# Pooled attention and a residual MLP on one core: batch 0's prologue regrouped, batch 1's v loaded in another shape, PSUM split into three pools

## The chip, the cores and the metric

The kernel runs on one core of one Trainium2 chip. The core has TensorE (PE, matrix products), VectorE (DVE), ScalarE (ACT), GpSimd (POOL) and SyncE (SP), each with its own instruction stream that it works through in order, and DMA engines that all of them share. Times are microseconds on the device. The metric is the time of one execution, lower is better.

## The reference, cut to what matters

There are 8 batches, 8 heads, 576 tokens and 64 values a head. Keys and values are averaged over groups of 8 tokens, so each query attends to 72 groups. Attention's output, 576 x 512 for a batch, then goes through a residual MLP that mixes tokens first and channels second:

```python
k_p = k.reshape(B, H, 72, 8, D).mean(axis=3);  v_p = v.reshape(B, H, 72, 8, D).mean(axis=3)
attn = softmax(scale * q @ k_p.T);  x = (attn @ v_p) laid out as (B, 576, 512)
a1 = alpha1 * x + beta1
u = x + lam * einsum('ts,bsd->btd', w_tok, a1)
a2 = alpha2 * u + beta2
out = u + lam * (relu(a2 @ w_ch1) @ w_ch2)      # 512 -> 2048 -> 512
```

Inputs and outputs are fp32. The products run in bf16 or fp16 with fp32 sums.

## The kernel before, in words

**Stages.** The tokens of a batch are cut into four chunks of 128 rows (token 4p + c lies on partition p of chunk c) and a remainder of 64; the remainders of two batches share a chunk. Four chunks make a block of the MLP, so there are nine blocks. A prologue (lines 659 to 748) does the attention and the token mix of batch 0 and prepares `w_tok`, biases and constants. Then block n of the MLP runs while the attention and the mix of batch n + 1 are woven into it.

**What sets the order.** Nothing is scheduled by a tool. The prologue is a written list of calls. In the loop over blocks each piece of work has a due number (`todo.append((at, ...))`), the list is sorted, and the pieces are issued in that order. Within a block, numbers 0 to 15 are the 16 columns of the first layer (`mlp_A`, L603), 16 to 31 are the 16 parts of the second layer (`mlp_B`, L619). Each engine follows its own stream; a wait at one instruction holds all that stand behind it on that engine.

**Attention of a batch.** `att_F` (L353) transposes q: for batches 0 and 1 by TensorE, later by DMA. `att_K` (L396) pools k with products by `pool_main` and `pool_rem`. For batch 0, `att_S` (L447) makes the scores of one head in two column halves and takes their exponentials; it uses `kpT_pool`, where the two halves of the partitions are kept apart with zeros. For the other batches `att_S4` (L463) makes four heads at once from `kp_pool`, with two half-array products side by side, and six exponentials (L503). For batch 0, `first_V` (L423) pools v by products of a 16-bit copy; for the others `att_V` (L438) adds fp32 v, eight tokens a partition on 72 partitions, in three VectorE sums a head pair (L442, L444). `att_AV` (L507) multiplies exponentials by pooled v (L518, L522); a column of eights beside v gives the sum for the division (L524, L526). `att_X` and `rest_X` (L536, L529) multiply by lambda times alpha1 and give `xs` in bf16, heads two by two.

**Mix and MLP.** `mix_T` (L565) multiplies the transposed `w_tok` by `xs` in five products of 512 columns (L572), adds x (L576), and multiplies by alpha2 (L579, `u_bf`). `mix_uT` (L581) transposes `u_bf` into `u_fm`: by TensorE for block 0, by DMA later. `mlp_A` is four products (L609) and a relu on ScalarE (L614). `mlp_B` is four products a part (L643) and, after the fourth part, two VectorE operations (L649, L650) and the store.

**Constants.** `spread_lam` (L275) copies lambda to all partitions by a K=1 product, `spread_al1` (L281) multiplies it by alpha1, `load_al2` (L271) broadcasts alpha2 by DMA from SP's queue. `setup_wtok` (L293), `setup_rowsum` (L306), `setup_vectors` (L288) and `setup_bias` (L343) prepare the transposed `w_tok`, its row sums and the biases. `keep_warm` (L559) issues products of 512 columns whose result nobody reads.

**Buffers and queues.** PSUM has eight banks. Six are the pool `psA` (`gp`, L52), handed out in turn to whatever asks; two are `psB`. A tile must wait until the last reader of the tile that held its bank is done. Loads that change the type go through POOL's queue, in the order of POOL's stream; stores, fp32 loads and DMA transposes go through SP's.

Of the kernel before, what the change touches and what calls it, by code (L numbers as in the profile page):

```python
# [14 lines left out]
P = 128  # L15
# [8 lines left out]
def kernel(  # L24
# [24 lines left out]
    psA = ctx.enter_context(tc.tile_pool(name="psA", bufs=6, space=bass.MemoryType.PSUM))  # L49
    psB = ctx.enter_context(tc.tile_pool(name="psB", bufs=2, space=bass.MemoryType.PSUM))  # L50

    def gp(name):  # L52
        return psA.tile([P, 512], FP, tag="gp", name=name)

# [61 lines left out]

    def load_rem(b, queue=nc.sync, behind=None):
# [52 lines left out]
    def load_wtok():  # L170
        nc.gpsimd.dma_start(out=wt_bf[:, 0:4 * S],
                            in_=moe_w_tok[0:512, :].rearrange("(p c) s -> p (c s)", c=4))
        nc.vector.memset(wt_bf[:, 5 * S:], 0.0)
        nc.vector.memset(wt_bf[64:128, 4 * S:5 * S], 0.0)
        nc.gpsimd.dma_start(out=wt_bf[0:REM, 4 * S:5 * S], in_=moe_w_tok[512:576, :])

# [3 lines left out]
    b2row = const.tile([4, P], FP, tag="b2row", name="b2row")  # L180
# [18 lines left out]
    nc.scalar.dma_start(out=b2row, in_=moe_beta2.rearrange("(c p) -> c p", p=P))  # L199
# [32 lines left out]
    vp1_pool, kpT_pool, kp_pool, ET_pool = [], [], [], []  # L232
    for i in range(4):
# [3 lines left out]
        if i < 2:  # L237
            t = const.tile([P, 2, 4, SPG], BF, tag=f"kpT_{i}", name=f"kpT_{i}")
            nc.vector.memset(t, 0.0)
            kpT_pool.append(t)  # L240
# [15 lines left out]
    def bias_row(i):  # L256
        p0 = 64 - 64 * i
        nc.vector.tensor_tensor(out=xs_pool[i][p0:p0 + 1, 4, :], in0=vecs[p0:p0 + 1, 1],
                                in1=vecs[p0:p0 + 1, 0], op=ALU.mult)

    b2c_bf = const.tile([P, 4], BF, tag="b2c_bf", name="b2c_bf")
    wtT = const.tile([P, 6, 640], BF, tag="wtT", name="wtT")
# [8 lines left out]
    def load_al2(behind):  # L271
        behind.memset(al2_bc[:, 0:1], 0.0)
        nc.sync.dma_start(out=al2_bc, in_=moe_alpha2.unsqueeze(0).to_broadcast((P, DM)))

    def spread_lam():  # L275

        ps = gp("ps_bc")
        nc.tensor.matmul(out=ps, lhsT=ones_row, rhs=vecs[0:1, 0])
        nc.scalar.copy(out=lam_bc, in_=ps)

    def spread_al1(half):  # L281

        ps = gp("ps_bc")[:, 0:256]
        cols = slice(256 * half, 256 * half + 256)
        nc.tensor.matmul(out=ps, lhsT=ones_row, rhs=vecs[0:1, 2, cols])  # L285
        nc.vector.tensor_tensor(out=lamal_bc[:, cols], in0=lam_bc[:, cols], in1=ps, op=ALU.mult)

    def setup_vectors():  # L288
        ps = gp("ps_vec")
        nc.tensor.transpose(out=ps[:, 0:4], in_=b2row, identity=identity[0:4, 0:4])  # L290
        nc.scalar.copy(out=b2c_bf, in_=ps[:, 0:4])

    def setup_wtok(tcx, copy):  # L293
# [4 lines left out]
        ps_w = gp("ps_w").bitcast(BF)  # L298
# [7 lines left out]
    def setup_rowsum(tcx):  # L306
# [3 lines left out]
        ps = gp("ps_rs")  # L310
# [32 lines left out]
    def setup_bias(g):  # L343
        ps_bias = gp("ps_bias")
# [8 lines left out]
    def att_F(b, hp, copy=nc.scalar.copy):  # L353
# [11 lines left out]
        ps_q = gp("ps_q").bitcast(BF)  # L365
# [30 lines left out]
    def att_K(b, u, copy):  # L396

        st = st1[b]
        ps_kp = gp("ps_kp")
# [18 lines left out]
        for a in range(2):  # L418
            rows = slice(64 * a, 64 * a + 64)
            (copy or (nc.scalar.copy, nc.vector.tensor_copy)[a])(  # L420
                out=kpT_pool[u][rows, a], in_=kp[rows])

    def first_V(b, u, copy=nc.vector.tensor_copy):  # L423
# [5 lines left out]
        for c in range(4):  # L429
            nc.tensor.matmul(out=vp, lhsT=pool_v, rhs=main[:, heads, c], start=(c == 0), stop=False)  # L430
        for c in range(2):
            nc.tensor.matmul(out=vp, lhsT=pool_vr, rhs=rest[:, heads, c], start=False,
                             stop=(c == 1))
# [13 lines left out]
    def att_S(b, h):  # L447
        st = st1[b]
        u, r, hh = h // 4, h // 2 % 2, h % 2
        ET = ET_pool[u][:, h % 4]  # L450
        for half in range(2):
            n0, n = 256 * half, 256 + 64 * half
            ps_sc = gp("ps_sc")
            nc.tensor.matmul(out=ps_sc[0:SPG, 0:256], lhsT=kpT_pool[u][:, half, h % 4, :],  # L454
# [406 lines left out]
```

The softmax here doesn't subtract the row's maximum and nothing guards it: scores larger than these inputs give would overflow.

## Time and profile before

The median of three runs is 346.46 us (346.36 to 346.72). The profiled execution took 345.48 us, and its span on the core is 343.8 us.

| Part of the profile | Reading |
|---|---|
| TensorE busy | 337.1 us, 98% of the span |
| VectorE, ScalarE, GpSimd busy | 224.7, 146.9, 90.2 us |
| Chain that ended last | PE 95%, of it first layer 36%, second layer 35%, token mix 11% |
| DMA | 45.77 MB, 133 GB/s over the span; 193 to 266 GB/s from 6.5 to 69.4 us |
| TensorE clock granted | 1.00 in every stage |

To read it: busy time of TensorE is modelled and includes the time in which a product drains, so it is checked against the distance between starts. The chain of work that ended last runs from the end backwards to whatever released each step. The stages of the table of windows were cut by hand: batch 0's attention (to 19.8 us), batch 0's mix (to 33.8), block 0's first layer, and so on.

### The profile page before, as it was taken

The numbers are of one execution on the slowest core, as the hardware profiler recorded it, in microseconds if no ns is written. First come the engines' busy times: TensorE is split into PE (matmuls) and PEld (weight loads), VectorE is DVE, ScalarE is ACT, GpSimd is POOL, SyncE is SP. The second block draws the span as 40 slices with busy tenths as digits, with TensorE's granted clock in tenths as the row PEclk, the third lists the DMA queues.
The fourth block names the chain that finished last, engine by engine and source line by source line (L and its number), as shares of the span: only waits on it lengthen the run. The fifth ranks groups of instructions, "written<-read, shape, count | busy, mean of one in ns | idle before, by whom it ended". The sixth has DMA issues, their size and how long they took to land.

```text
span 343.8 us, 5902 instructions
## 1 busy us (share of the span) xinstructions
PE 337.1 (98%) x2221; PEld 177.4 (52%) x2221; DVE 224.7 (65%) x476; ACT 146.9 (43%) x277; POOL 90.2 (26%) x105
## 2 busy tenths in 40 slices
PE   8999999999999999999999999999999999999995
PEld 3667654455445544555445544554455445545544
DVE  6664579985787667866867598768675881037511
ACT  3655980068205830385028500880089006604700
POOL 8768507201144012701170117002600200000000
PEclk9999999999999999999999999999999999999999
DMA  8999999968678907794479437982810132011012
GB/s 123 184 222 287 215 202 248 188 139 130 161 210 172 194 2 192 150 225 54 129 200 213 65 110 179 204 131 63 241 41 1 48 76 78 0 61 62 2 54 68
DMA packets 66654, 45.77 MB, mean 133 GB/s; under 512 B 34457, under 2 KB 57373, under 8 KB 66626
## 3 DMA queue, kind: packets, MB, share of 16 engines
q1 hardware_dynamic: 51716, 32.73, 40.2%
q0 software_dynamic: 14448, 12.40, 22.6%
q8 instruction: 17, 0.28, 0.3%
q10 hardware_dynamic: 462, 0.27, 0.3%
q14 instruction: 11, 0.09, 0.1%
HBM read 38.30 MB, written 9.44 MB: 139 GB/s over the span
## 4 chain that ended last, share of the span: by engine, by line
PE 95%; DMA 2%; ACT 1%; DVE 1%; issue 0%; ACTq 0%; POOLq 0%
PE ps_h L609 36%; PE ps_ch L643 35%; PE ps_tok L572 11%; PE ps_s L474 2%; PE ps_av L518 2%; DMA q_bf<-in_q_dram 2%; PE ps_ch L632 1%; PE ps_kp L404 1%; PE ps_warm L563 1%; PE ps_q L367 1%; PE ps_sc L454 1%; PE ps_r L481 1%; PE ps_av L522 1%; PE ps_bias L348 0%; PE ps_bc L285 0%
## 5 line engine op out<-in xcount | busy, mean ns | idle before, releaser
L614 ACT ACTIVATE Hj<-ps_h,bias_cols 128x512 bf16<-128x512 f32 x144 | 98.3, 689 | 164.4 <-PE ps_h L609 163.1
L609 PE MATMUL ps_h<-u_fm,w 128*128 128x512 bf16 (+1 forms) x592 | 133.3, 374 | 0.2 <-ACT u_fm L595 0.2
L643 PE MATMUL ps_ch<-w,Hj 128*128 128x512 bf16 x560 | 130.9, 379 | 0.0
L609 PEld LDWEIGHTS <-w 128*128 128x128 bf16 x592 | 63.8, 114 | 51.7 <-issue 3.0
L643 PEld LDWEIGHTS <-Hj 128*128 128x128 bf16 x560 | 52.9, 98 | 61.6 <-issue 1.6
L572 PE MATMUL ps_tok<-xs,wtT 128*128 128x512 bf16 (+3 forms) x200 | 44.9, 380 | 0.3 <-DVE xs L540 0.3
L649 DVE TENSOR_TENSOR ps_ch<-lam_bc,ps_ch 128x512 f32<-128x512 f32 x32 | 22.2, 693 | 33.3 <-PE ps_ch L643 33.0
L540 POOL TENSOR_TENSOR xs<-x_tm,lamal_bc 128x512 bf16<-128x512 f32 x10 | 12.7, 1269 | 112.5 <-DVE x_tm L526 110.4
L576 DVE TENSOR_TENSOR u_sb<-x_tm,ps_tok 128x512 f32<-128x512 f32 (+1 forms) x40 | 27.4, 684 | 10.6 <-PE ps_tok L572 10.5
L524 DVE RECIPROCAL rec<-ps_av 128x5 f32<-128x5 f32 x64 | 12.2, 191 | 32.5 <-PE ps_av L522 32.4
L526 DVE TENSOR_TENSOR x_tm<-ps_av,rec 128x320 f32<-128x320 f32 x64 | 31.5, 492 | 2.7
L650 DVE TENSOR_TENSOR u_sb<-u_sb,ps_ch 128x512 f32<-128x512 f32 x35 | 24.0, 687 | 13.6 <-PE ps_ch L643 12.5
L503 ACT ACTIVATE ET<-ps_s 72x512 f16<-72x512 f32 x56 | 32.3, 592 | 0.0
L442 DVE TENSOR_TENSOR v_u<-v_u 72x512 f32<-72x512 f32 (+1 forms) x56 | 30.8, 550 | 1.0
L572 PEld LDWEIGHTS <-wtT 128*128 128x128 bf16 (+3 forms) x200 | 17.4, 100 | 21.3 <-issue 1.7
L579 DVE TENSOR_TENSOR u_bf<-u_sb,al_bc 128x512 bf16<-128x512 f32 x34 | 26.7, 785 | 1.7 <-DMA u_fm<-u_bf 0.6
L162 POOL TENSOR_TENSOR k_raw<-k_raw 128x512 f32<-128x512 f32 x14 | 18.3, 1310 | 9.1 <-DMA k_raw<-in_k_dram 6.5
L164 POOL TENSOR_TENSOR k_bf<-k_raw 128x512 bf16<-128x512 f32 x14 | 18.4, 1318 | 1.1
L518 PEld LDWEIGHTS <-ET 72*128 72x128 f16 x256 | 14.1, 97 | 8.7 <-DVE vp L435 0.2
L79 POOL DMA_DIRECT2D q_bf<-in_q_dram x16 | 12.6, 788 | 16.7 <-DVE v_u L136 15.2
L540 DVE TENSOR_TENSOR xs<-x_tm,lamal_bc 128x512 bf16<-128x512 f32 x22 | 15.4, 701 | 0.7
L518 PE MATMUL ps_av<-vp,ET 72*128 72x66 f16 x256 | 15.8, 193 | 0.0
(121 smaller groups left out, 214.9 us busy)
## 6 DMA issues: line engine op xcount, KB each, us to landing
out_dram<-u_sb SPq DMA_DIRECT2D x32, 256.0 KB
k_raw<-in_k_dram SPq DMA_DIRECT2D x12, 512.0 KB
v_u<-in_v_dram SPq DMA_DIRECT2D x12, 512.0 KB
q_bf<-in_q_dram POOLq DMA_DIRECT2D x16, 256.0 KB, 6.6
w<-in_moe_w_ch_dram POOLq DMA_DIRECT2D x8, 512.0 KB, 14.6
v_u<-in_v_dram POOLq DMA_DIRECT2D x2, 576.0 KB, 15.1
k_raw<-in_k_dram POOLq DMA_DIRECT2D x2, 512.0 KB, 15.9
rem_raw<-in_q_dram SPq DMA_DIRECT2D x15, 64.0 KB
```

What stands on the lines that cost most here:

```text
L442: nc.vector.tensor_tensor(out=t[:, :, 0:n], in0=t[:, :, 0:n], in1=t[:, :, n:2 * n], op=ALU.add)
L503: nc.scalar.activation(out=o, in_=i, func=AF.Exp, bias=0.0, scale=0.125)
L518: nc.tensor.matmul(out=av[:, odd + c, :], lhsT=ET[:, m0:m0 + 128], rhs=vp1[:, hh, :])
L526: nc.vector.tensor_tensor(out=x[:, 1 - odd:6 - odd, dd:dd + D], in0=av[:, :, 0:64], in1=rec.unsqueeze(2).to_broadcast((P, 5, D)), op=ALU.mult)
L540: eng.tensor_tensor(out=xs[:, 0:4, cols], in0=x[:, 1:5, cols], in1=lamal_bc[:, cols].unsqueeze(1).to_broadcast((P, 4, D * (h1 - h0))), op= ...
L572: nc.tensor.matmul(out=ps_tok[p0:p1], lhsT=wtT[0:kk, at, P * c:P * c + p1 - p0], rhs=xs_pool[i][0:kk, sc, :], start=(sc == 0), stop=(sc == 4))
L576: nc.vector.tensor_tensor(out=s["u"][p0:p1, :], in0=x[p0:p1, 1 + c if c < 4 else 5 - 5 * i, :], in1=ps_tok[p0:p1, 0:DM], op=ALU.add)
L579: eng.tensor_tensor(out=s["u_bf"], in0=s["u"], in1=al2_bc, op=ALU.mult)
L609: nc.tensor.matmul(out=ps_h[:, t0:t1], lhsT=w1_of(cc, j), rhs=u_fm[n][:, cc, t0:t1], start=(cc == 0), stop=(cc == 3))
L614: nc.scalar.activation(out=t, in_=ps_h, func=AF.Relu, bias=bias_cols[:, j:j + 1], scale=1.0)
L643: nc.tensor.matmul(out=ps, lhsT=Hj[n, j][:, 128 * m:128 * m + 128], rhs=w2[j // 4][:, j % 4, :], start=(j == 0), stop=(j == NJ - 1))
L650: nc.vector.tensor_tensor(out=u, in0=u, in1=ps, op=ALU.add)
```

## The change

Four things change together.

1. **Batch 0's attention.** `att_S` and `kpT_pool` go; batch 0 uses `att_S4`, heads 0 to 3 and then 4 to 7, with all six exponentials of a group directly behind. `att_AV` comes in the order 2, 3, 0, 1, 4 to 7. Lambda times alpha1 is multiplied in one row first and then spread (`spread_lamal`). The token mix of batch 0 is cut into column halves, heads 0 to 3 and 4 to 7 (`mix_half`, eight times four products of 256 columns), and the fifth product of each chunk comes after (`mix_T`). Chunks 1 and 3 are transposed as fp32 and scaled by alpha2 in the copy (`mix_uT_fp`). There are 22 unread products instead of 16, twelve of them at the start.
2. **Batch 1's v.** It is loaded as fp32 with four tokens a partition (`load_v32`; the last 64 tokens with two), VectorE adds four to one (`sum_v`), and `first_V` pools the result by two products for four heads. In block 0 the heads of batch 1 come later (dues 14.0 to 19.0 instead of 11.9 to 18.7), the second layer's first two parts are done for all four chunks before the rest, and batch 1's own chunks are transposed by TensorE.
3. **Loads.** alpha2 goes into POOL's queue behind `w_tok`; lambda is broadcast by SP's queue. Batch 1's k, both last quarters of w1, and batch 1's v move in POOL's stream.
4. **PSUM.** `psA` has four banks, `psB` two, and a new `psX` two, which take the scores' second pairs, `mlp_B`'s chunks 2 and 3, heads 2 and 3 of the later batches and several set-up tiles.

```diff
-    psA = ctx.enter_context(tc.tile_pool(name="psA", bufs=6, space=bass.MemoryType.PSUM))
+    psA = ctx.enter_context(tc.tile_pool(name="psA", bufs=4, space=bass.MemoryType.PSUM))
     psB = ctx.enter_context(tc.tile_pool(name="psB", bufs=2, space=bass.MemoryType.PSUM))
+    psX = ctx.enter_context(tc.tile_pool(name="psX", bufs=2, space=bass.MemoryType.PSUM))
...
+    def load_v32(b):
+        main = work.tile([P, H, 4, D], FP, tag="v_u", bufs=2, name="v_main")
+        rest = work.tile([32, H, 2, D], FP, tag="v_u", bufs=2, name="v_rest")
+        nc.gpsimd.dma_start(out=main.rearrange("p h c d -> p h (c d)"),
+                            in_=v[b, :, 0:512, :].rearrange("h (p c) d -> p h (c d)", c=4))
...
+    def sum_v(b, u):
...
+        m = main[:, 4 * u:4 * u + 4]
+        nc.vector.tensor_tensor(out=m[:, :, 0:2], in0=m[:, :, 0:2], in1=m[:, :, 2:4], op=ALU.add)
+        nc.vector.tensor_tensor(out=vs[:, 4 * u:4 * u + 4, 0], in0=m[:, :, 0], in1=m[:, :, 1],
+                                op=ALU.add)
...
+        nc.gpsimd.dma_start(out=al2_bc, in_=moe_alpha2.unsqueeze(0).to_broadcast((P, DM)))
...
+    nc.vector.tensor_tensor(out=vecs[0:1, 2], in0=vecs[0:1, 2], in1=vecs[0:1, 0], op=ALU.mult)
...
+    def load_lam(behind):
+        behind.memset(lam_bc[:, 0:1], 0.0)
+        nc.sync.dma_start(out=lam_bc, in_=moe_lam.unsqueeze(0).to_broadcast((P, DM)))
+
+    def spread_lamal(half, copy):
+        ps = bp("ps_bc")[:, 0:256]
+        cols = slice(256 * half, 256 * half + 256)
         nc.tensor.matmul(out=ps, lhsT=ones_row, rhs=vecs[0:1, 2, cols])
+        copy(out=lamal_bc[:, cols], in_=ps)
...
+        ps_av = (xp if b > 1 and h in (2, 3) else gp)("ps_av")
...
+    def mix_half(c, half):
+        if half == 0:
+            ps_mix[c] = gp("ps_tok")
+        cols = slice(256 * half, 256 * half + 256)
+        for sc in range(4):
+            nc.tensor.matmul(out=ps_mix[c][:, cols], lhsT=wtT[:, sc, P * c:P * c + P],
+                             rhs=xs_pool[0][:, sc, cols], start=(sc + half == 0), stop=False)
...
+    def mix_uT_fp(c):
+        ps = xp("ps_uT")
...
+            nc.tensor.transpose(out=ps[:, 128 * cc:128 * cc + 128],
+                                in_=st2[0, c]["u"][:, 128 * cc:128 * cc + 128], identity=identity)
...
+            nc.vector.tensor_scalar(out=u_fm[0][:, cc, 128 * c:128 * c + 128],
+                                    in0=ps[:, 128 * cc:128 * cc + 128],
+                                    scalar1=al2c[:, cc:cc + 1], scalar2=None, op0=ALU.mult)
...
-        if blk:
+        if key[0] > 1 or key == (0, 4):
             nc.sync.dma_start_transpose(out=u_fm[blk][:, :, 128 * at:128 * at + 128],
                                         in_=s["u_bf"])
...
     new_batch(1)
     for g in range(2):
         load_w1(g)
+    bias_row(0, nc.gpsimd)
     load_q_bf(1, 0)
     load_q_bf(1, 1)
-    for u in range(2):
-        load_k(1, u, queue=nc.gpsimd)
-    keep_warm(3)
-    spread_lam()
-    keep_warm(3)
+    keep_warm(12)
     att_F(0, 0)
     att_F(0, 1)
     cast_rem(0, nc.vector)
+    spread_lamal(0, nc.scalar.copy)
...
+    scores(0)
     first_V(0, 0)
     double_k(1)
+    spread_lamal(1, nc.scalar.copy)
+    att_AV(0, 2)
+    att_K(0, 1, None)
+    att_F(0, 2, bank=xp)
+    att_F(0, 3, nc.vector.tensor_copy, xp)
+    att_AV(0, 3)
+    att_X(0, 2, 4, nc.gpsimd)
+    scores(1)
...
+    mix_uT_fp(1)
+    setup_bias(0, bp)
     mix_uT((0, 0))
+    mix_uT_fp(3)
     mlp_A(0, 0, 0, 256)
     mix_uT((0, 2))
...
-            for i, dt in enumerate((2.9, 3.4, 4.6, 5.1) if u else (5.7, 6.2, 2.9, 3.4)):
+            late = ((6.0, 6.5, 5.0, 5.5), (3.9, 4.4, 4.9, 5.4))[u]
+            for i, dt in enumerate(late if first else (2.9, 3.4, 4.6, 5.1) if u else (5.7, 6.2, 2.9, 3.4)):
...
+        if first:
+            for u in (0, 2, 1):
+                todo.append((11.0 + 0.1 * u, lambda u=u: sum_v(b, u)))
+            for u in range(2):
+                todo.append((13.2 + 1.0 * u, lambda u=u: first_V(b, u)))
...
-            at = 21.0 + 1.3 * c
+            at = (21.7 if first else 21.0) + 1.3 * c
...
-                at = 16 + 4 * m + part
+                at = 16 + (4 * part + m if n == 0 and part < 2 else 4 * m + part)
+                if n == 0 and part > 1:
+                    at = 24 + 2 * m + part - 2
```

## The prediction

> **What bounds the kernel now.** I read the page's first part, then the waits of TensorE, then the table of stages, then single stretches of the timeline.
>
> ```profile
> PE 337.1 (98%) x2221; PEld 177.4 (52%) x2221; DVE 224.7 (65%) x476; ACT 146.9 (43%) x277; POOL 90.2 (26%) x105
> PE ps_warm L563 <- DVE warm L201: 1.4, 1, 1.4
> PE ps_rs L312 <- ACT wtT L303: 0.3, 1, 0.3
> PE ps_tok L572 <- DVE xs L540: 0.3, 1, 0.3
> PE ps_h L609 <- ACT u_fm L595: 0.2, 1, 0.2
> ```
>
> TensorE is the bound, and its waits add up to almost nothing. A share of busy time flatters it, so I checked the starts: five products of 512 columns take 1.08 us of the chain (0.216 each), and from 33.8 us on the starts follow at that pace with some 0.3 us lost. So after the prologue every added product lengthens the kernel, and only the prologue (to 33.8) has air in it. The stages:
>
> ```profile
> 6.50:19.80 13.30, 12.83 (x140) 9.00 (x141) 8.73 (x31) 8.07 (x23) 9.78 (x13) 1.00 1.29 193
> 19.80:33.80 14.00, 13.16 (x160) 10.21 (x157) 8.27 (x16) 8.02 (x18) 11.21 (x14) 1.00 1.21 266
> 33.80:46.20 12.40, 12.40 (x131) 7.72 (x129) 6.47 (x16) 11.50 (x26) 5.66 (x7) 1.00 1.10 214
> 46.20:55.20 9.00, 8.93 (x76) 4.79 (x76) 8.26 (x29) 4.59 (x10) 2.08 (x2) 1.00 1.11 222
> 55.20:69.40 14.20, 14.20 (x71) 6.28 (x70) 12.87 (x18) 0.00 (x0) 6.54 (x7) 1.00 0.99 197
> ```
>
> Columns are stretch, PE, PEld, DVE, ACT, POOL, clock, DMA share, GB/s. The reader should see two things: DMA is full through all of it, and VectorE is nearly full (8.26 of 9.00) just ahead of 55.2. The timeline shows how near that is:
>
> ```profile
> 33.82 0.61 PE L367 MATMUL ps_q<-identity_bf,q_bf 128*128 128x128 bf16 x8
> 44.13 0.30 PE L518 MATMUL ps_av<-vp,ET 72*128 72x66 f16 x4
> 53.50 0.18 DVE L524 RECIPROCAL rec<-ps_av 128x5 f32<-128x5 f32 x1
> 53.72 0.49 DVE L526 TENSOR_TENSOR x_tm<-ps_av,rec 128x320 f32<-128x320 f32 x1
> 54.25 0.69 DVE L540 TENSOR_TENSOR xs<-x_tm,lamal_bc 128x512 bf16<-128x512 f32 x1
> 55.18 1.24 PE L572 MATMUL ps_tok<-xs,wtT 128*128 128x512 bf16 x5
> 69.44 4.48 PE L609 MATMUL ps_h<-u_fm,w 128*128 128x512 bf16 x20
> ```
>
> Batch 1's last `xs` ends at 54.94 and the product that needs it starts at 55.18. That is 0.24 us of slack. I call 33.82 S (four feed-forward columns of block 0 and the first two biases are issued, batch 1's q transposes begin), 44.13 the first attention product of batch 1, 55.18 M (its first token mix), 69.44 the end of block 0.
>
> [...]
>
> **The prologue.** Twelve unread products replace six and a K=1 product: 1.40 + 12 x 0.43 = 6.56 at most, and q lands at 1.31 + 5.17 = 6.48, so nothing moves. The K=1 product of 256 columns (0.62, L285) now stands before the remainder transposes and the row product before the cast (0.68, L258 shape); the first scores start at 10.5 instead of 9.87[...]. This hardly matters, because two landings pin what follows: the second q at 6.83 + 6.6 = 13.4 and `w_tok` at 8.29 + 9.2 = 17.5. Scores in fours make twelve exponentials of sixteen; a half takes ScalarE 2 x 0.175 + 4 x 0.48 by their starts at 76.6 and 86.9. The halves' scores start at 10.5 and, behind the second q (0.45 for transposes, 0.2, a 0.59 copy), at 14.6; the last exponential ends at 17.4, and the `w_tok` transposes start at 17.65 instead of 19.76. The sums for `xs` don't hold the mixing: POOL issues its loads until 14.3 (al2's 0.57, the bias row's 1.3 at most, and q, whose issue waits for an earlier landing as it does at 12.35 today), then makes heads 2 and 3 from 15.45, heads 0 and 1 until 18.8, heads 4 and 5 until 20.1; VectorE makes the last pair until 20.8. The first half is mixed from 19.1, the second from 21.5.
> From there to S TensorE has: transposes of `w_tok` 5 x 0.28 = 1.4; two heads 0.3; mixing in halves 8 x 0.44 + 4 x 0.22 = 4.4; row sums 4 x 0.28 = 1.1; vectors 0.2; fp32 transposes 8 x 0.15 = 1.2; biases 2 x 0.53 = 1.1; bf16 transposes 2 x 0.22 = 0.4; feed-forward 32 x 0.109 = 3.5. Sum 13.6. An fp32 transpose of this size is not in the trace: not under the bf16 one's 0.055, not over the 0.31 between fp32 passes of 256 columns (L285); I take 0.15 from the small one (L290), keeping 0.4 to 2.5 for eight. Waits: 0.4 for `ps_vec`, whose bank is freed by the third of four 0.69 us copies on ScalarE; 0.4 for the second fp32 set, whose bank is freed when VectorE has made four scaled copies (1.0 by L435's 0.24 spacing, the nearest row) behind the fourth residual add; some 0.3 of hand-overs. S = 17.65 + 13.6 + 1.1 = 32.3. Range 30.9 (no wait, cheapest transposes) to 33.1. Gain 1.5.
>
> **Block 0.** Added on TensorE after S: batch 1's v pooled by products, four of 256 columns with two changes of row count each side, 4 x 0.107 + 4 x 0.09 = 0.8; sixteen transposes of `u_bf` that DMA did before, 16 x 0.055 = 0.9. S to the first pooling product: as before from 33.82 to 46.27, less two heads (0.3) and a mode change: 12.1. So 44.4.
> Does v arrive? Before: second k 15.36 + 15.9 = 31.3, third w1 quarter 34.4, v 36.7 and 39.7, last w1 quarter 41.9. Now the last quarter (2.2) is ahead of v and one more 256 KB broadcast is under way (alpha2 joins POOL's queue ahead of w1, lambda takes its place on SP's): 256 KB at 266 GB/s, 1.0. v as 128-partition rows like k (512 KB in 1.4 to 1.9) takes 3.3 instead of 5.3. Landing 31.3 + 1.0 + 3.1 + 2.2 + 3.3 + 0.4 = 41.3, ends 40.3 and 43.0. VectorE then adds 2 x (0.69 + 0.42) + 0.69 = 2.9: ready at 44.2, just in time. Behind that wait on VectorE stand only v's copies and the heads, so nothing else is held.
> First head of batch 1: 44.4 + 0.4 + scores 0.9 + one column 0.86 = 46.55. From here two engines race to M. TensorE has eight heads 8 x 0.15, pooling 0.4, one column 0.86, six parts of the second layer 6 x 0.864 = 5.2: 7.7. VectorE's work before, from 44.49 to 54.94, was 10.45; less 0.23 idle and less `att_V`'s last pair (0.68 + 0.42 + 0.29, 1.48 by starts) it is 8.74; two new v copies bring 0.48, and the first evacuation starts 0.36 after its head: 9.6. M = 56.15. **TensorE waits 1.9 us there**: the later heads removed columns that had covered VectorE.
> M to the end was 14.26; with the transposes 15.1. End of block 0: 71.25 against 69.44, **+1.8**. Check by terms: -1.5 + 0.8 + 0.9 + 1.9 - 0.3 (block 0's old losses).
>
> **Later blocks, at nothing.** With four banks in the first pool, column j7 needs the bank whose relu ended at 75.86 + 0.69 = 76.55; it starts at 76.63. All other tiles of a block have more. The two scores' halves and the third and fourth output chunk alternate in the new pool with 10 us between. The reordered second layer, four open sums, has its last weights 2.5 us and more before use. POOL's k sums (35.1 and 38.2, behind six load issues) are ready 1.0 and 0.4 ahead of their products.
>
> The sum stands against its own span of 343.8; the three timed runs are 346.36 to 346.72, so I add 1.8 to their median: 348.3.
>
> **Rivals.**
> 1. VectorE doesn't bind at M[...]. Then M comes at 46.55 + 7.7 and the sum is -0.1: 346.4, no change. For: TensorE waits nowhere on VectorE there today. Against: 0.24 us of slack today and 2.9 us less cover.
> 2. Faster: the prologue gives more. Work after 17.5 could be 13.0 with no wait, S = 30.5 at best, and if M isn't bound either, 67.6 + 0.0: 344.6. With the wait at M it turns faster only with S before 30.4.
> 3. v lands at 43.0 or later: pooling waits until 45.9, and everything behind it shifts by 1.5: 349.8. For: DMA share above 1.1 throughout.
> 4. The banks do bind: 0.1 to 0.2 us at j7 and j14 in seven blocks, +1.5 on top, 349.8. Against: each release above precedes its use.
>
> **How the numbers follow.** Theory 0.60 (alone 347.2 to 349.2: S from 30.9 to 33.1 moves it, v's readiness damps the low side), rival 3 0.11, rival 4 0.05, rival 1 0.13, rival 2 0.11. About 0.7 us (0.2%) is what a measurement of this kernel can tell from no change. Faster is rival 2, the same is rival 1, slower the rest, 0.76. The range goes from 346.2 (rival 1 inside, rival 2 out) to 349.9.
>
> **What would show it.** TensorE's waits must list `ps_tok` on DVE `xs` with 1.5 to 2 us near 56; S, the first q transposes of batch 1, near 32.3; v's sums starting on VectorE near 41.3 after idling on DMA; blocks 1 to 7 as long as before (35.2 from 69.44 to 104.66). Wrong if S is before 31, if `xs` doesn't appear as a releaser, or if blocks 1 to 7 differ.

## The result, and the profile after

| | Before | Changed |
|---|---|---|
| Median, us | 346.59 (346.36 to 347.44, 4 runs) | 351.20 (349.89 to 352.77, 4 runs) |
| Ratio | 1 | 1.013 (95% interval 1.0082 to 1.0178) |
| Profiled execution: time, span | 345.48, 343.8 | 349.89, 348.2 |
| S, M, end of block 0 | 33.82, 55.18, 69.44 | 33.31, 57.66, 72.81 |
| Last matmul's start to the end of the span | 4.03 | 5.09 |

Slower, as forecast (348.3), but by 4.6 us instead of 1.8. The same changed kernel run once more on another chip, later in this study, took 348.83 against 346.38: 1.0074 (1.0060 to 1.0088), or 2.45 us. So there are two questions: where the mechanism cost more than forecast, and what came and went between the two measurements.

The forecast's terms against the two profiles (times since the start of the span; each row is the change against the profile before):

| Stretch, change in us | Forecast | First profile | Repetition |
|---|---|---|---|
| Start to S | -1.5 | -0.51 | -0.42 |
| S to M | +2.5 | +2.99 | +2.99 |
| M to the end of block 0 | +0.8 | +0.89 | +0.89 |
| Later blocks | 0 | 0 | 0 |
| Behind the last matmul | 0 | +1.05 | +0.17 |
| Sum | +1.8 | +4.4 | +3.6 |

The repetition's 3.6 is a difference of spans; its medians differ by 2.45 only. The profile before was one of the faster executions of its kernel (345.48 us beside a median of 346.46) and that of the repetition one of its slower ones (349.25 beside 348.83), so the difference of the two profiles comes out high. The forecast added the profile's 1.8 us to a median; that the repetition's median then lies only 0.5 us from it, with the terms 1.8 us apart, is in part luck.

The page's first part of the changed kernel:

```profile
PE 335.2 (96%) x2222; PEld 179.4 (52%) x2261; DVE 221.4 (64%) x475; ACT 146.8 (42%) x276; POOL 92.7 (27%) x109
```

TensorE has less busy time than before (335.2 against 337.1) in a longer span: the loss is waiting. Its waits (columns: us in total, times, longest):

```profile
PE ps_tok L603 <- DVE xs L559: 1.7, 1, 1.7
PE ps_warm L582 <- DVE warm L234: 1.4, 1, 1.4
PE ps_bc L312 <- DVE vecs L286: 0.9, 1, 0.9
PE ps_uT L619 <- ACT u_fm L640: 0.7, 1, 0.7
...
PE ps_q L395 <- DMA q_bf<-in_q_dram: 0.3, 1, 0.3
...
PE ps_q L395 <- ACT qT L400: 0.2, 1, 0.2
```

The first line is the wait that the prediction put its name to. The third was not forecast at all. By stages, cut at the same events as before (columns: stretch, its length, busy time of PE, PEld, DVE, ACT and POOL with counts, clock, DMA share, GB/s):

```profile
6.70:18.80 12.10, 10.35 (x138) 7.00 (x140) 7.39 (x27) 7.58 (x19) 9.50 (x14) 1.00 1.29 205
...
46.20:57.60 11.40, 9.71 (x86) 5.24 (x86) 8.91 (x33) 4.40 (x10) 1.90 (x2) 1.00 0.81 156
57.60:72.80 15.20, 15.03 (x84) 7.21 (x87) 12.49 (x18) 2.34 (x4) 6.97 (x7) 1.00 0.58 144
```

The clock column counts from the clock's first record on, at 7.36 here and 8.95 before; ahead of it the unread products of 512 columns start 0.43 us apart in both profiles, twice the 0.216 of later ones. So a 1.00 in the first row, here and before, leaves the opening out.

In the row from 46.20 TensorE is idle for 1.69 of 11.40 us. VectorE shows why only in the timeline:

```profile
33.31 0.61 PE L395 MATMUL ps_q<-identity_bf,q_bf 128*128 128x128 bf16 x8
47.92 0.28 PE L537 MATMUL ps_av<-vp,ET 72*128 72x66 f16 x4
56.29 0.49 DVE L545 TENSOR_TENSOR x_tm<-ps_av,rec 128x320 f32<-128x320 f32 x1
56.82 0.69 DVE L559 TENSOR_TENSOR xs<-x_tm,lamal_bc 128x512 bf16<-128x512 f32 x1
57.66 1.24 PE L603 MATMUL ps_tok<-xs,wtT 128*128 128x512 bf16 x5 [1.67 <-DVE xs L559]
72.81 4.48 PE L654 MATMUL ps_h<-u_fm,w 128*128 128x512 bf16 x20
```

Behind the first head of batch 1 (47.92) VectorE has no gap over 0.1 us from 48.3 on, and the mix starts right behind its last full `xs` (56.82 + 0.69). From 72.81 to the start of block 2 at 108.01 it is 35.20 us, before 35.22; every later block keeps its length within 0.02 us.

The 1.05 us at the end stand in the timeline as a longer stretch behind VectorE's last add. Before, with the span ending at 343.8:

```profile
340.05 0.42 DVE L637 TENSOR_TENSOR u_sb<-u_sb,ps_ch 128x256 f32<-128x256 f32 x1 [1.33 <-PE ps_ch L632]
```

Changed, ending at 348.2:

```profile
343.40 0.42 DVE L682 TENSOR_TENSOR u_sb<-u_sb,ps_ch 128x256 f32<-128x256 f32 x1 [1.33 <-PE ps_ch L677]
```

The DMA view of the changed kernel from 343.5 to 348.2 (GB/s in 40 slices, then a queue with packets, MB and share):

```profile
GB/s 244 270 148 35 0 0 0 139 0 0 0 0 70 166 209 210 227 157 18 9 9 0 17 9 17 0 0 0 0 0 0 0 0 0 0 0 0 0 0 0
...
q8 instruction: 1, 0.02, 1.7%
```

One packet of 16 KB moves through an instruction queue (q8) here, from 344.42 for 1.31 us. That it is a part of TensorE's program is my reading; the trace names the queue alone. All but the last two of the final store's landings are in by 346.03. Its last eight packets of 1 KB start only as the fetch ends, from 345.72 on, and go out one after another (the 9s and 17s); the last landing is at 346.95. In the repetition, without a fetch, it is at 346.15.

### The profile page after: what moved, and what is told of

It is laid out like the page before. It is cut to its first block, busy times and chain, and to the rows that moved or that the text cites. A ratio compares the mean times of both kernels' runs of the same rounds, so it can differ in the third digit from the quotient of the medians.

```text
span 348.2 us, 5934 instructions
## 1 busy us (share of the span) xinstructions
PE 335.2 (96%) x2222; PEld 179.4 (52%) x2261; DVE 221.4 (64%) x475; ACT 146.8 (42%) x276; POOL 92.7 (27%) x109
## 4 chain that ended last, share of the span: by engine, by line
PE 90%; DVE 4%; ACT 2%; DMA 1%; issue 1%; ACTq 1%; DVEq 0%
PE ps_h L654 34%; PE ps_ch L688 33%; PE ps_tok L603 11%; PE ps_s L489 3%; PE ps_av L537 2%; DMA vecs<-in_moe_alpha_dram 1%; DVE x_tm L545 1%; PE ps_ch L677 1%; PE ps_tok L592 1%; PE ps_kp L432 1%; PE ps_r L496 1%; PE ps_warm L582 1%; DVE xs L559 1%; PE ps_bias L376 1%; ACT wtT L331 1%
## 5 line engine op out<-in xcount | busy, mean ns | idle before, releaser
L688 PE MATMUL ps_ch<-w,Hj 128*128 128x512 bf16 x543 | 128.5, 379 | 1.0 <-issue 0.5
L603 PE MATMUL ps_tok<-xs,wtT 128*128 128x512 bf16 (+3 forms) x184 | 41.4, 380 | 1.9 <-DVE xs L559 1.7
L522 ACT ACTIVATE ET<-ps_s 72x512 f16<-72x512 f32 x64 | 36.4, 593 | 0.0
L472 DVE TENSOR_TENSOR v_u<-v_u 72x512 f32<-72x512 f32 (+1 forms) x48 | 26.4, 550 | 0.8
L603 PEld LDWEIGHTS <-wtT 128*128 128x128 bf16 (+3 forms) x184 | 15.9, 100 | 20.9 <-issue 3.8
L611 DVE TENSOR_TENSOR u_bf<-u_sb,al_bc 128x512 bf16<-128x512 f32 x32 | 24.9, 777 | 1.3 <-DMA u_fm<-u_bf 0.3
L86 POOL DMA_DIRECT2D q_bf<-in_q_dram x16 | 12.6, 788 | 17.6 <-DVE v_u L167 16.8
```

Of the source, the lines that this page charges most:

```text
L472: nc.vector.tensor_tensor(out=t[:, :, 0:n], in0=t[:, :, 0:n], in1=t[:, :, n:2 * n], op=ALU.add)
L522: nc.scalar.activation(out=o, in_=i, func=AF.Exp, bias=0.0, scale=0.125)
L603: nc.tensor.matmul(out=ps_tok[p0:p1], lhsT=wtT[0:kk, at, P * c:P * c + p1 - p0], rhs=xs_pool[i][0:kk, sc, :], start=(sc == 0), stop=(sc == 4))
L611: eng.tensor_tensor(out=s["u_bf"], in0=s["u"], in1=al2_bc, op=ALU.mult)
L688: nc.tensor.matmul(out=ps, lhsT=Hj[n, j][:, 128 * m:128 * m + 128], rhs=w2[j // 4][:, j % 4, :], start=(j == 0), stop=(j == NJ - 1))
```

## Experiments

My theory after the result had four parts: VectorE sets M; the row product of lambda and alpha1 delays the start; the fetch lengthens the end; and the timed runs lose clock, because three of the four runs of the changed kernel had a granted clock of 0.990 to 0.993 while the profiled one had 1.00.

**Later mixes.** In `attention`:

```diff
-            at = (21.7 if first else 21.0) + 1.3 * c
+            at = (23.7 if first else 21.0) + 1.3 * c
```

> The changed kernel with batch 1's five token mixes and their transposes 2.0 positions later in block 0's order, so that two more sets of channel products (0.87 us each) stand ahead of the first mix; no work is added or taken away. Theory (VectorE sets the first mix): the 1.67 us that TensorE waits for VectorE's last product of batch 1 is filled, block 0 ends near 71.1 instead of 72.81 in the profile and the time falls by 1.5 to 1.7 us. Rival (the block's end is set by something behind the mix, such as the transposes of the last chunks in front of block 1, or the wait only moves there): block 0 ends within 0.4 us of 72.81 and a new wait of over 1 us stands at the first products of block 1.

Measured: 348.30 against 346.31, ratio 1.0054 (1.0039 to 1.0068). Timeline:

```profile
57.48 1.24 PE L603 MATMUL ps_tok<-xs,wtT 128*128 128x512 bf16 x5
...
70.90 0.81 PE L654 MATMUL ps_h<-u_fm,w 128*128 128x512 bf16 x3
```

The mix starts just behind VectorE as before, but TensorE no longer stood idle. From S (33.15) to the end of block 0 it is 37.75 us instead of 39.50, and no new wait came at block 1. The medians don't show it cleanly, since 13 of these 20 runs lost some clock; the seven that kept it (0.997 or more) have a median span of 345.2 us, the repetition of the changed kernel 346.95. VectorE at M is shown, with its 1.7 us.

**Row products behind the scores.**

```diff
-    nc.vector.tensor_tensor(out=vecs[0:1, 2], ...)        # was ahead of the k copies
...
     att_K(0, 0, None)
+    nc.vector.tensor_tensor(out=vecs[0:1, 2], ...)
...
-    spread_lamal(0, nc.scalar.copy)                       # was ahead of att_Frem
...
+    spread_lamal(0, nc.scalar.copy, gp)
     spread_lamal(1, nc.scalar.copy)
```

> The changed kernel with VectorE's product of lam and alpha1 behind the first pooled keys in its order, and both row products on TensorE behind the first scores. Theory (the row product, which waits for alpha1 to land, is what made the start 1 us later than forecast): TensorE's wait of 0.94 us at the first row product is gone, the first scores start near 10.3 instead of 11.21, w_tok's transposes near 17.9 instead of 18.80 (the first part of w_tok lands at 17.6), S near 32.4 instead of 33.31, and the time falls by 0.8 to 0.9 us. Rival (q, which landed 0.5 us later than in the kernel before, sets the start, and the other inputs behind it in the same queue set the rest): the first scores move, but w_tok's transposes stay within 0.3 us of 18.80 and the time within 0.3 us.

Measured: 349.33, ratio 1.0081 (1.0055 to 1.0107). The first scores moved to 9.77, further than expected, yet `w_tok`'s transposes started at 19.03. The table of stretches says why (the third number from the end is the granted clock):

```profile
9.96:13.37 3.41, 3.09 (x39) 2.04 (x35) 2.38 (x7) 2.90 (x8) 3.21 (x5) 1.00 1.46 204
13.37:16.78 3.41, 3.41 (x47) 2.91 (x44) 1.91 (x6) 1.76 (x5) 1.86 (x3) 0.50 1.09 226
```

The clock fell to half for 3.41 us. Neither theory nor rival had that; it ate the gain. The rival's sign, transposes within 0.3 us of 18.80, came true for another reason than the rival's. This profile turned the question to the clock.

**Narrower unread products, and one less.** Two ways to move the fetch. The first:

```diff
-    keep_warm(12)
+    keep_warm(48, 128)        # 128 columns each
```

> The changed kernel with the first twelve unread products of 512 columns written as 48 of 128 columns: the same columns in all, but 72 more instructions in TensorE's program. Theory (a fetch of 16 KB of TensorE's program falls into the last store of the output and holds it up): the fetch comes some 36 of the last half-width products earlier, about 4 us, ahead of the last store, and the stretch from the start of the last matmul to the end falls from 5.09 us to about 4.05 us, as in the kernel before; the time falls by about 1.0 us if the start keeps its times. Rival (the last store's landing varies by chance, or the longer tail belongs to something else that changed): the stretch stays at 5.1 us, or the fetch moves and the stretch does not.

The second:

```diff
     rest_X(0, 0, 2, nc.gpsimd)
-    keep_warm(2)
+    keep_warm(1)
     setup_wtok(0, nc.scalar.copy, xp)
```

> The changed kernel with one unread product less (the second of the two ahead of w_tok's transposes), so that TensorE's program is two instructions shorter. Two kernels with the longer tail (the changed one, and the one with later mixes) have one instruction more on TensorE than one without it (the one with later row products). Theory (the last block of TensorE's program is fetched into the final store, and one more instruction calls for it): no fetch of 16 KB at the end, the stretch from the start of the last matmul to the end is 4.0 to 4.2 us instead of 5.09, and the time falls by about 1.0 us, up to 0.2 more from the product itself. Rival (tail by chance): the stretch is 5.1 again or any value between, and the time falls by 0.2 us at most.

The fetch moved to 335.3 in the first and is not there in the second, and the end took 4.19 and 4.18 us. But the times were 350.20, ratio 1.0092 (1.0057 to 1.0128), and 351.33, ratio 1.0135 (1.0089 to 1.0180). In both profiles the clock fell in the start, once and twice (mean granted clock 0.994 and 0.990), and S came at 34.55 and 35.64. The end behaved as expected, the time did not.

**The kernel before with a longer program.** Thirteen of its unread products are cut up:

```diff
-    keep_warm(3)
+    keep_warm(3, 4)           # each in four parts; eleven in four, two in two
```

> The kernel before, with eleven of its unread products cut into four each and two into two: the same columns, 70 instructions more on TensorE, which makes its program one instruction longer than that of the changed kernel. Theory (the fetch): a fetch of 16 KB now falls into the last store, the stretch from the start of the last matmul to the end grows from 4.03 to about 5.1 us, and the time rises by about 1.0 us with S within 0.3 of 33.82. Rival (the tail belongs to something else in the changed kernel): the stretch stays at 4.0 to 4.2 us and the time within 0.4 us of before.

Measured: 346.93, ratio 1.0010 (0.9996 to 1.0024); the end took 4.01 us, and the fetch came at 345.2, when the program was over. S was 34.74, outside what was expected, with the clock open only at 11.1. My rule that the count of instructions decides fell here.

**The changed kernel once more.**

> The changed kernel as it is, on another chip. If the extra microsecond at the end belongs to the program (a fetch of 16 KB that starts 1.3 us after the start of the last matmul), it stands there again: 5.1 us from the start of the last matmul to the end, with the fetch in the records. If it was chance, 4.0 to 4.2. If the clock is lost[...], most runs again have 0.995 or less, with medians of 350 to 352; if that belonged to the first chip, all have 1.0 and about 349.5.

Measured: 348.83, ratio 1.0074 (1.0060 to 1.0088). S 33.40, M 57.75, end of block 0 72.90, as in the first profile within 0.1 us. But no fetch in the last store, 4.20 us at the end, and a clock of 0.997 or more in all four runs. So the wait at M belongs to the program, the microsecond at the end does not. Of 18 profiles two have the fetch inside the last store (this kernel's first and the one with later mixes), with 5.09 and 5.08 us; the other 16 have 3.95 to 4.22. What puts it there stays open. That the loss of clock belongs to one chip is excluded too: kernels with this start lost it on three chips in the other runs.

**Batch 1's v as before.** All due numbers of block 0 are those of the kernel before, too; start, pools and TensorE's transposes stay as changed.

```diff
-    for g in range(2, 4):
-        load_w1(g)
-    load_v32(1)
+    load_w1(2)
+    for u in range(2):
+        load_v(1, u, (2,), queue=nc.gpsimd)
+    load_w1(3)
...
+        for i, hp in enumerate((1, 0, 2, 3) if first else range(4)):
+            todo.append(((6.6, 8.7, 10.0, 12.6)[i] if first else 0.2 + 2.0 * hp, lambda hp=hp: att_V(b, hp)))
```

> The changed kernel with batch 1's v as it was before: eight tokens a partition, pooled by VectorE alone, its loads ahead of the fourth group of channel weights, with the positions of the kernel before for v, heads, token mixes and channel products in block 0. Kept are the start, the three pools and batch 1's transposes on TensorE. Theory (the new v path with its later heads costs the 1.67 us wait and some 1.4 us of products around it): S stays near 33.3, the first token mix starts near 54.7 (33.31 plus the 21.36 of the kernel before), block 0 ends near 69.8 instead of 72.81, and the time falls by 3.0 us, by 4 if the fetch at the end goes too. Rival (the start's new order of loads or the three pools hold block 0 back): the first mix stays above 56.5 and the time falls by less than 1.5 us.

Measured: 348.64, ratio 1.0060 (1.0033 to 1.0088). S itself was late (35.16, the clock fell at 10.0), so I count from it: 22.9 us to M, where the kernel before took 21.36. TensorE's waits name the reason:

```profile
PE ps_bc L312 <- DVE vecs L286: 1.7, 1, 1.7
...
PE ps_ch L688 <- DMA w<-in_moe_w_ch_dram: 0.7, 1, 0.7
```

There is also 0.6 us on TensorE's weight loads for w1. In this trace v lands at 39.3 and 42.5 us and the last quarter of w1 behind it at 45.6; in the kernel before these were 36.7, 39.7 and 41.9. VectorE doesn't wait for v, but TensorE waits for the weights. Half of the 2.99 us came back (1.4), against an expectation of all of it, so the rival was right in part: the order of loads decides the other half. Going back to the old v in this order of loads trades VectorE's wait for waits on weights.

**Full rows and one row in the wait.** Five unread products in the wait for the row product, once with 128 rows and once with one row:

```diff
     cast_rem(0, nc.vector)
+    keep_warm(5)             # second kernel: the same with warm[0:1] on both sides
     spread_lamal(0, nc.scalar.copy)
```

> The changed kernel with five more unread products of 128 rows (1.08 us at full clock) where TensorE waits 0.9 to 1.7 us for the row product. Theory[...]: the clock is 1.0, or 0.997 at least, in every timed run instead of 0.99 and 0.993, the spans scatter by under 0.8 us, and the median falls from 351.2 to about 349.5 to 350.2, although work is added. Rival (the clock is lost elsewhere, or by the chip): the clock stays at 0.99 to 0.995 in most runs and the time at 351 or above.

> As the run before it, but the five added products use one row of the array instead of 128: the same stretch of time on TensorE, next to no work in it. Theory of rows[...]: the added products don't help, the clock is 0.995 or below in most runs as in the changed kernel, and the median is 0.8 us or more above the one with full products. Theory of time[...]: the clock is 1.0 in every run, as with full products, and the two agree within 0.4 us.

Measured, full rows: 349.24, ratio 1.0086 (1.0056 to 1.0117), clock 0.998 to 1.0 in four of four. One row: 350.25, ratio 1.0116 (1.0079 to 1.0152), clock 0.994 or 0.995 in three of four. The stretches are as long as the 3.41 us at half clock in the run with late row products; full rows first:

```profile
4.22:7.63 3.41, 2.49 (x18) 1.22 (x17) 0.89 (x3) 1.89 (x4) 3.34 (x8) 1.00 1.28 196
7.63:11.04 3.41, 2.33 (x26) 1.19 (x25) 1.90 (x9) 0.98 (x3) 3.41 (x6) 1.00 1.44 179
```

One row:

```profile
6.20:9.61 3.41, 2.99 (x21) 1.42 (x20) 2.00 (x10) 1.37 (x4) 3.41 (x6) 1.00 1.46 196
9.62:13.03 3.41, 3.05 (x34) 1.98 (x35) 0.52 (x3) 0.76 (x4) 3.13 (x4) 0.50 1.41 184
```

With one row TensorE was busy for 2.99 of 3.41 us, and the next 3.41 us ran at half clock; with full rows it was busy for 2.33 of 3.41 us in one stretch and the clock stayed at 1.00. So the share of busy time alone doesn't tell the two apart. The kernel with full rows is 1 us faster than the one with the same products of one row, though the two intervals overlap; it is no faster than the repetition of the changed kernel (348.83), which kept its clock without them.

The two edits differ in nothing but the rows of five products, and the clock held in four of four runs of one and in one of four of the other. What of TensorE's work makes the clock fall is not shown.

**Two edits, then three.** The five products and the later mixes:

> The changed kernel with two of the edits tried so far together: five unread products in the wait for the row product, and batch 1's token mixes 2.0 positions later. Theory (the lost clock and VectorE at the first mix are separate costs and add): no wait for VectorE at the first mix, from S to the end of block 0 37.7 to 37.8 us as with later mixes alone (39.5 in the changed kernel), clock 0.997 or more in every run, and a median of 347.3 to 347.7, 1.7 below the run with the products alone. Rival (one cost hides the other): less than 0.8 us below it.

Measured: 347.48, ratio 1.0049 (1.0031 to 1.0067), clock 0.997 to 1.0 in all five runs, S to the end of block 0 37.76: as expected. Then the row products late, the mixes late, and three unread products in the bank of `first_V`:

```diff
         ps_v = gp("ps_v")
+        for _ in range(fill):     # 3 for batch 0's first call
+            nc.tensor.matmul(out=ps_v, lhsT=warm[:, 0:P], rhs=warm)
```

> The changed kernel with the row products behind the first scores, batch 1's token mixes 2.0 positions later, and three unread products of 128 rows ahead of the first product that pools v, where the clock fell when the row products alone were moved. Theory (the wait for alpha1 makes the start late, and the earlier run of this edit hid it by losing the clock for one window): clock 0.997 or more in every run, first scores at 9.7 to 10.0, w_tok's transposes at 17.6 to 18.1, S at 32.3 to 32.8, and a median of 346.4 to 347.0, about 1 us below the run before it. Rival (S is set by landings and by the work behind w_tok alone): S stays at 33.1 or later and the median within 0.4 us of the run before it.

Measured: 347.32, ratio 1.0041 (1.0026 to 1.0057). First scores 9.45, `w_tok`'s transposes 17.82, all as the theory has it, and S where the prediction had put it:

```profile
27.20 0.66 PE L619 MATMUL ps_uT<-identity,u_sb 128*128 128x128 f32 x4 [0.68 <-ACT u_fm L640]
...
32.34 0.61 PE L393 MATMUL ps_q<-identity_bf,q_bf 128*128 128x128 bf16 x8
```

The profile's end of block 0 is 0.70 us earlier than in the run before it (70.11 against 70.81); the medians differ by 0.16, which their spread does not resolve. The median missed what was expected of it (346.4 to 347.0), so that S came earlier is shown by the profile alone.

**Batch 1's transposes by DMA.** In the first kernel on top of the last run, with other positions; in the second alone:

```diff
-        if key[0] > 1 or key == (0, 4):
+        if blk:
             nc.sync.dma_start_transpose(...)
...
-                todo.append((at + (2.6 if first and c < 4 else 1.8), lambda key=key: mix_uT(key)))
+                todo.append((at + 1.8, lambda key=key: mix_uT(key)))
```

> As the run before it, but batch 1's v products and heads 1.0 position earlier, its mixes 1.0 later than in the changed kernel instead of 2.0, and its chunks transposed by DMA, as in the kernel before, in place of sixteen transposes on TensorE. Theory (sixteen transposes cost TensorE 0.9 us that DMA gives for nothing): from the first mix to the end of block 0 14.2 to 14.4 us instead of 15.15, no wait for VectorE at the first mix above 0.3 us, block 0 ends at 69.2 to 69.7, a median of 345.6 to 346.3, below the kernel before or equal to it. Rival (the transposes by DMA come too late or wait for the loads of batch 2): a wait on u_fm at the first columns of block 1 of 0.5 us or more, and no gain on the run before it.

> The changed kernel with batch 1's chunks transposed by DMA as before, nothing else. Theory: from the first mix to the end of block 0 14.2 to 14.4 us instead of 15.15, 0.8 to 0.9 us off the profile at the end of block 0 counted from S, with the wait for VectorE at the first mix still 1.5 to 1.9 us and the clock still lost in most runs. Rival (the transposes on TensorE lie beside something else that bounds the stretch): 15.0 us or more.

Measured: 351.72, ratio 1.0173 (1.0152 to 1.0194), and 350.73, ratio 1.0150 (1.0126 to 1.0174). In both kernels the first columns of block 1 wait, as the first one's rival had it. In the second kernel they wait for the transposes:

```profile
PE ps_h L654 <- DMA u_fm<-u_bf: 2.4, 1, 2.4
```

The timeline of SP's queue in it:

```profile
71.26 0.36 SPq L697 DMA_DIRECT2D out_dram<-u_sb  x1
71.67 1.22 SPq L633 DMA_TRANSPOSE u_fm<-u_bf  x1
```

The last transpose stands behind a store on SP, and the store waits for its sum, which VectorE, busy without a gap from 65.8 on, ends at 71.24. From M to the end it is 16.8 us less the 2.4 of waiting: 14.4, so the sixteen transposes do cost 0.8, but DMA can't take them in this order. In the first kernel the wait is 4.4 us, and the clock was at half from 73.3 to 76.7. Its trace names one of VectorE's sums of v, which these products don't read, so what they waited for is not shown there.

**Work into the bank wait.** On top of the run with the row products late: the second biases and the fifth part of `w_tok` ahead of `mix_uT_fp(3)`, one unread product less:

```diff
     mix_uT((0, 0))
+    setup_bias(1, bp)
+    setup_wtok(4, nc.scalar.copy, bp)
     mix_uT_fp(3)
```

> The run with late row products, later mixes and three unread products, with two more edits: the second group of biases and the fifth part of w_tok's transposes go into the 0.68 us that TensorE waits ahead of the second pair of fp32 transposes, and one unread product less stands ahead of w_tok's transposes. Theory (the wait is for a bank, and work put there is free): no wait there, S near 31.6 to 31.8 instead of 32.34, block 0 ends at 69.3 to 69.6, and the median is 0.6 to 0.9 us below that run's, which is the time of the kernel before within 0.5 us. Rival (the copies on ScalarE or the column weights hold what follows, and the wait comes back later): S within 0.2 us of 32.34 and the time within 0.3 us of that run's.

Measured: 346.40, ratio 0.9997 (0.9979 to 1.0016). S was 31.61 as expected, but block 0 ended at 70.22: v was late. To see whether by chance, once more, beside a kernel with lambda's 256 KB behind v (and v's rest summed ahead of its second half):

```diff
-    load_lam(nc.vector)
...
+            todo.append((12.0, lambda: load_lam(nc.vector)))
...
-                todo.append((2.6 + 0.9 * hp, lambda hp=hp: att_F(b, hp, bank=xp)))
+                todo.append((2.6 + 0.9 * hp, lambda hp=hp: att_F(b, hp, bank=(xp, xp, gp, gp)[hp])))
```

> The run with biases in the wait once more, beside the run before it on the same chip. If its v lands late by the loads ahead of it and not by chance, VectorE's sums of v start again at 42.0 to 42.8 and block 0 ends near 70.2; its median is within 0.3 us of the kernel before.

> The run with biases in the wait, and three more edits: the 256 KB of lam, first used behind the second layer, are loaded at position 12 of block 0 instead of ahead of v; v's short rest is summed before its second half; the third and fourth set of batch 1's q transposes use the large pool. Theory (once S is early, v's landing sets block 0, and bytes ahead of v move it): v's sums start near 41.4 instead of 42.40, TensorE no longer waits for v's rest (0.8 us) nor for ScalarE's copies at the third set (0.4 us), block 0 ends at 69.0 to 69.4 instead of 70.22 (69.44 in the kernel before), and the median is 0.6 to 1.1 us under that run's on the same chip. Rival (v is held by loads other than lam, or VectorE's chain of heads starts no earlier): v's sums start after 42.0 and block 0 ends after 69.9.

The first of VectorE's sums of v, in the first run of it:

```profile
42.40 0.69 DVE L144 TENSOR_TENSOR v_main<-v_main 128x512 f32<-128x512 f32 x1 [3.23 <-DMA v_main<-in_v_dram]
```

and in its repetition:

```profile
40.48 0.69 DVE L144 TENSOR_TENSOR v_main<-v_main 128x512 f32<-128x512 f32 x1 [1.16 <-DMA v_main<-in_v_dram]
```

With lambda behind v it starts at 40.43.

The 2 us were chance, and lambda's bytes don't move v: my reading of the first run fell. Block 0 ended at 69.72 and 69.61. The medians are 346.09 and 345.80 against 346.26, ratios 1.0001 (0.9984 to 1.0018) and 0.9986 (0.9972 to 1.0000). The last is the best version found. It is level with the kernel before, since its interval reaches 1; the changed kernel is clearly beaten.

## Why the prediction was right and wrong

The mechanism at M was right; the start was wrong, and the clock and the end stood in the sum at nothing.

- **TensorE waits for VectorE at M: right.** Forecast 1.9 us, 1.67 by the list of waits (1.84 by the starts). First head to M 9.74 against 9.6, pooling to first head 2.19 against 2.15, M to the end of block 0 15.15 against 15.1. Shown by the run with later mixes.
- **S at 32.3: a wrong step.** It came at 33.31, one microsecond of the gain gone. The step said that the order of the first products "hardly matters, because two landings pin what follows". In the first profile they did not: the second q landed at 13.48 and the first part of `w_tok` at 17.59, as forecast, but TensorE came to them 0.95 and 1.2 us later, held up by its own work.

```profile
7.99 0.68 DVE L286 TENSOR_TENSOR vecs<-vecs 1x512 f32<-1x512 f32 x1 [1.47 <-DMA vecs<-in_moe_alpha_dram]
8.72 0.69 PE L312 MATMUL ps_bc<-vecs,ones_row 1*128 1x256 f32 x2 [0.94 <-DVE vecs L286]
11.21 0.30 PE L489 MATMUL ps_s<-qT,kp 64*72 64x256 bf16 x2
14.43 0.61 PE L395 MATMUL ps_q<-identity_bf,q_bf 128*128 128x128 bf16 x8
18.80 0.72 PE L328 MATMUL ps_w<-identity_bf,wt_bf 128*128 128x128 bf16 x10
```

The first scores were forecast for 10.5 and started at 11.21, `w_tok`'s transposes for 17.65 and started at 18.80. So 0.7 us were lost ahead of the scores and 0.4 behind them. The row product was put down at 0.68 us of VectorE work and nothing for alpha1's landing, which VectorE waited 1.5 us for and TensorE 0.9 (0.4 to 1.7 in other profiles). With the row products moved and the clock kept, S was 32.34. From `w_tok` to S the sum was near: 14.5 against 14.7, with fp32 transposes at 0.11 each for 0.15, and 0.68 for the bank instead of 0.4. The range given for S, 30.9 to 33.1, is narrower than its own terms: the cheapest transposes with no wait give 30.45, the dearest with all waits 33.65. In the repetition the two landings were later (14.45 and 18.53), only just ahead of TensorE, so there a leaner start would have gained less.
- **Banks at nothing: right for the later blocks, wrong in block 0.** Seven blocks keep their length within 0.02 us. But the third set of batch 1's q transposes waits for ScalarE's copy of the first, as these sets share the new pool of two banks: 0.38 us by the starts. S to the first pooling product took 12.42 instead of 12.1, about this wait. With the third and fourth set in the large pool it is gone from the list of waits, and this stretch is 12.38 against 12.62 in the run beside it.
- **The end: not in the prediction.** 1.05 us in that execution. The trace shows the fetch in front of the last packets; the repetition of the kernel had neither. Whether the three timed runs beside the profile had it is not known.
- **The clock: a term put at nothing without a reason.** The profile before has 1.00 in every stage of the table, and the prediction took that for the new start without asking. Every timed run of the first measurement beside the profiled one was at 0.993 or 0.990. In the run with later mixes, which had 20, the span had a median of about 345.2 us with the clock at 0.997 or more and 346.5 where it was 0.995: a fall of the clock to that mean is worth some 1.3 us. Over the kernels that keep the start of the changed one (itself twice, and the runs with later mixes, narrower products, one product less, the old v, transposes by DMA), 27 of 45 runs were under 0.996; over those that fill the gap with full products, or move the row products and fill elsewhere, 3 of 62, not counting the one that lost it in a wait at block 1. That this made up the rest of the first measurement is argued from these, since its timed runs left no trace of where the clock fell. The repetition kept it with waits of 1.35 us for q and 1.29 for the row product in its start; why it did is not shown.

Of the rivals, v did not come late in the changed kernel's profiles: VectorE's sums of it start at 40.7 and 42.3, and the first pooling product 12.42 us behind S in both. The new pools didn't cost the later blocks anything. The rival that VectorE doesn't bind is excluded. The faster one needed S near 30.5 and no wait at M, or S before 30.4.

## What to carry to other kernels

When a woven schedule is moved, look first for the engine whose chain of small steps races the bound engine to the next meeting point, and keep other work ahead of that point: moving the mixes by two places gave back 1.7 us for nothing. Look at the granted clock of every run, too: with the early wait for the row product left bare, three of the first four runs had 0.990 to 0.993, and in the run with late row products one fall to half speed lasted 3.41 us. Five full-row products in that wait went with 0.998 to 1.0 in four of four runs, so where runs lose clock, fill such a wait, or move what waits behind work that is ready. And measure a kernel more than once before explaining the last microsecond of it: a fetch and the clock were worth some 2 us in the first measurement and were not there in the second.

## What the runs showed of the hardware

- **The clock can fall in the middle of work.** In the run with late row products it was at half for 3.41 us (13.37 to 16.78), right behind 3.41 us in which TensorE was busy for 3.09. With five one-row products in the wait it fell behind a stretch with 2.99 us busy; with five full-row products it stayed at 1.00 behind one with 2.33. The clock opened at 7.36, 8.95 and 11.1 us in the profiles of the changed kernel, the kernel before and the latter with a longer program. It does not fall in every execution of one program: 13 of 20 runs with later mixes had less than 0.997, seven had 0.997 or more.
- **An instruction fetch can stand ahead of the last packets.** The instruction queue q8 moved 18 packets of 16 KB in the first profile of the changed kernel. The one inside the last store took 1.31 us, and the end took 5.09 us; the other profile with one there has 5.08, the 16 without 3.95 to 4.22. The other 17 packets held up nothing that the list of waits shows: what it puts down to issue on TensorE is 0.5 us in all.
- **fp32 transposes** of 128 x 128 took 0.11 us of TensorE each in the changed kernel's profile (starts from 26.15 on), twice the 0.055 of the bf16 ones (from 27.11 on).
- **Landings scatter.** The same program's v was there for VectorE at 42.4 us in one execution and at 40.5 in another, 1.9 us apart; `w_tok` landed at 17.6 and 18.5 in the two profiles of the changed kernel.
